# HGRN2 attention with an ELU MLP on one core: the first unit's last pair gets gates of its own, dummy products fill waits of the lead-in, and the order of the lead-in changes

## The chip, the core and the metric

The kernel runs on one core of one Trainium2 chip. The metric is device time in microseconds (us) of one execution; lower is better. The core has five engines with instruction queues of their own, each run strictly in order: TensorE (PE, with its weight loads as PEld), VectorE (DVE), ScalarE (ACT), GpSimd (POOL) and SyncE (SP), which here only starts transfers. Engines wait for each other by semaphores. Results of TensorE go to PSUM, whose banks carry names (tags) such as m0, m3, a0, a1 and h.

## The reference, cut to what matters

```python
# q, k, v, f_logit: (4 batches, 8 heads, 768 tokens, 48), fp32
f = 1.0 / (1.0 + np.exp(-f_logit))
for t in range(S):
    state = f[:, :, t, :, None] * state + np.einsum('bhd,bhe->bhde', k[:, :, t], v[:, :, t])
    y[:, :, t] = np.einsum('bhd,bhde->bhe', q[:, :, t], state)
x = y.transpose(0, 2, 1, 3).reshape(3072, 384)
h = x @ w_in                                                  # 384 x 2048, 64-bit
g = np.where(h > 0.0, h, np.exp(np.minimum(h, 0.0)) - 1.0)
out = g @ w_out                                               # 2048 x 384, 64-bit
```

A gated recurrence runs over the tokens, and its output, with the heads side by side, goes through a two-layer MLP with the ELU function between the layers.

## The kernel before

**Units.** The 3072 tokens are cut into 12 units of 256, three to a batch. A unit passes through an attention part and an MLP part; the attention of later units is strewn into the MLP of earlier ones. The eight heads are four pairs, and `NKT` = 3 is the number of the last pair.

**Attention.** `gates` turns the logits into 1 + exp(-f) on ACT; `grow` makes a running product of them with a scan on DVE, and `fall` its reciprocal on DVE (the two slots of tile `f`). `scale` multiplies k with the running product and q with the reciprocal, pair by pair, on POOL. `transposed` turns k on TensorE and has ACT copy it out; `advance` multiplies k with v into the state's increments (banks a0, a1); `step` adds up the states of the four chunks of 64 tokens; `scores` multiplies q with k, and `mask` keeps the causal half; `outputs` and `carried` (for unit 0: `first_outputs`) make the attention's result x (tile `xt`).

To spare work on the gates, the logits of pair 3 are not given a pair's room of their own: their rows fill the gaps (32 partitions) that pairs 0 to 2 leave unused, so that three pairs' instructions handle all four. `move` then copies them with two transfers inside SBUF to where pair 3 belongs: once for the running product, once for its reciprocal.

**Weights.** They arrive as 64-bit numbers, in 16 pieces of 0.79 MB (eight of w_in, eight of w_out) in the order in which they are needed: wi0, wi1, wi2, wo0, wi3, wo1, wi4, wo2, wi5, wo3 and so on. `fetch(n)` loads piece n into slot n mod 7 of the buffer `area`; a piece of w_in takes three transfers, one of w_out a single one. `split` (two DVE operations), `lower` (one on ACT) and `merge` (one on DVE) turn it into 32-bit numbers. `merge(n)` ends with `fetch(n + AHEAD)`, `AHEAD` = 7, since its slot is free then. A transfer is also issued only when the one some eight before it has landed, because they share eight semaphores in turn.

**Order.** Everything is emitted in an order written by hand, and each engine runs its instructions in that order. First comes the lead-in (L1037 to L1114): loads, the attention of unit 0 and most of the gates of unit 1. Then a loop over steps T = 0 to 191 follows. Step T, for P = T / 2, first applies the ELU of an earlier product on even steps (`elu`, for units 0 and 1), then what `at_step` has planned for T, then `up(P)` on even steps (first MLP layer, L923 for units 0 and 1, L878 from unit 2) or `down(P - 2)` on odd ones (second layer, L955 and L977), then `split` and `lower` of the piece that is merged two steps later. `A1` gives the steps of unit 1's attention: its entries are those of transposes, advance, steps, scores and mask, outputs, carried. Unit 1 has P = 6, 7, 8 between unit 0's products.

**Queue of SP.** In the lead-in SP issues, in this order: f, k, q of unit 0; f of unit 1; v of unit 0; fetch(0); k, q, v of unit 1; fetch(1); the first move of unit 1; fetches 2 to 6; then fetch(7) from merge(0). The moves of unit 0, and the second of unit 1, go out on ACT's queue.

**Dummy products.** `warm(n)` multiplies the identity with itself n times over 512 columns into bank m3; nothing reads the result. There are three at the start (`W0`) and one (`WA`) before unit 0's first `advance`. Each fp32 product is two instructions on TensorE.

Of the kernel before, what the change touches and what calls it, by code (L numbers as in the profile page):

```python
# [8 lines left out]
FP32 = mybir.dt.float32  # L9
# [347 lines left out]
def fast(ctx: ExitStack, tc: tile.TileContext, q, k, v, f_logit, w_in, w_out, out, flag, outer):  # L357
# [38 lines left out]
    WA = 1  # L396
    W0 = 3
    HOLD = 2
    A1 = (2, 4, 4, 5, 7, 9)
# [28 lines left out]
    def load(u, names="fkqv"):  # L428
        b, s0 = u // UPB, (u % UPB) * U
        for n in names.replace("v", ""):  # L430
            to = qkf[u % NB][n][MAIN]
            frm = src[n][b, :, :, s0 : s0 + U].rearrange("(p r) d s -> (r d) p s", r=2)
            if n == "f":
                to, frm = to[:, 0:NKT, 0], frm[:, 0:NKT]
            nc.sync.dma_start(out=to, in_=frm)
            for r in range(2 if n == "f" else 0):
# [14 lines left out]
    def blank(i, *engines, zeros=None):  # L451
# [4 lines left out]
        (zeros or engines[-1]).memset(qkf[i]["f"][:, NKT], 1.0)  # L456
# [114 lines left out]
    def merge(n):  # L571
        if wide and n < NFT:
# [4 lines left out]
            nc.vector.tensor_tensor(out=to.bitcast(I32), in0=bits, in1=hi, op=ALU.add)  # L577
# [67 lines left out]
    def watch(u):  # L645
        nc.vector.scalar_tensor_tensor(
            out=fine[:], in0=qkf[u % NB]["f"][:, 0:NKT, 0, U - 1 :], scalar=LIMIT, in1=fine[:],
            op0=ALU.is_le, op1=ALU.mult,
        )
# [378 lines left out]
    def warm(n):  # L1028

        pw = ps.tile([128, 4, 128], FP32, tag="m3", name="psW")  # L1030
# [6 lines left out]
    gates(0, (1, 2))  # L1037
# [4 lines left out]
    warm(W0)  # L1042
    for p in range(NKT):
        grow(0, p)
        scale(0, ("k", p, nc.gpsimd))
        if p < 2:
            transposed(0, 0, "m0", (p,))
    move(0, 0, nc.scalar)
    transposed(0, 1, "m1", (0,))
    fall(0, 0)  # L1050
    scale(0, ("q", 0, nc.gpsimd))
    warm(WA)
# [8 lines left out]
    scale(0, ("k", NKT, nc.gpsimd), ("q", 1, nc.gpsimd))  # L1061
    fall(0, 2)
    move(0, 1, nc.scalar)
    transposed(0, 1, "m1", (1,))
    advance(0, (2,))
    scores(0, None, (1,), pc)
    scale(0, ("q", 2, nc.gpsimd))
    advance(0, (3,))
    scores(0, None, (2,), pc)
# [3 lines left out]
    )  # L1073
    a = qkf[1]["f"][:, 0:NKT, 0]
# [4 lines left out]
    scale(0, ("q", NKT, nc.gpsimd))  # L1079
    scores(0, None, (NKT,), pc)  # L1080
    fall(1, 0)
    for c in range(NC - 1):
        step(0, c)
    mask(0, pc)
    step(0, NC - 1)
    split(0)
# [8 lines left out]
    for n in range(HOLD, AHEAD):  # L1095
        fetch(n)
    fall(1, 1)
    first_outputs(0)
    lower(0)
    merge(0)  # L1100
    first_outputs(1)
    scale(1, ("k", 0, nc.gpsimd), ("q", 0, nc.gpsimd), ("k", 1, nc.gpsimd), ("k", 2, nc.gpsimd))
    scale(1, ("k", NKT, nc.gpsimd))
    split(1)
    transposed(1, 0, "a0")
    transposed(1, 1, "a1")
    lower(1)
    watch(0)
    scale(1, ("q", 1, nc.gpsimd))
    fall(1, 2)  # L1110
    scale(1, ("q", 2, nc.gpsimd))
    move(1, 1, nc.scalar)
# [98 lines left out]
```

## Time and profile before

| | |
|---|---|
| median of 10 runs (lowest, highest) | 569.57 us (567.3, 571.53) |
| the profiled execution: its time; its span | 571.33 us; 569.6 us |
| granted TensorE clock, mean over the span | 0.985 |
| busy: PE, PEld | 548.1 us, 502.6 us |
| busy: DVE, ACT, POOL | 394.8, 229.5, 265.1 us |
| first up(0), up(1), up(2) start (L923) | 31.67, 35.67, 40.20 us |
| first down(0) starts (L955) | 46.81 us |
| transfers to 60 us: bytes, mean rate | 14.21 MB, 237 GB/s |

The span runs from the first to the last instruction of the profiled execution. Busy times of engines overlap. A granted clock of 0.50 means that TensorE ran at half its rate in that stretch.

### The profile page before, as it was taken

Reading aid. Unit: us, or ns where it says so; the run is one execution under the profiler, and the core shown is the slowest. Engines: PE = TensorE matmul, PEld = TensorE weight load, DVE = VectorE, ACT = ScalarE, POOL = GpSimd, SP = SyncE. Lnnn points to the kernel's source line nnn. Section 1 sums busy time; section 2 is a strip of 40 time slices with the busy share of each in tenths; the row PEclk is TensorE's granted clock in tenths of the full one; section 3 lists DMA queues with packets and bytes.
Section 4 is the critical chain, followed back from the end, with each engine's and each line's share of the span. In section 5 each row is a group of like instructions: output and inputs, shape, how many; then the busy total and the mean of one; then the engine's idle time right before and its main releaser. Section 6 shows DMA issues by size and latency. Waiting matters only on the chain.

```text
span 569.6 us, 15170 instructions
## 1 busy us (share of the span) xinstructions
PE 548.1 (96%) x6210; PEld 502.6 (88%) x6210; DVE 394.8 (69%) x765; ACT 229.5 (40%) x417; POOL 265.1 (47%) x530
## 2 busy tenths in 40 slices
PE   5588999999999999999999999999999999999996
PEld 2465777778999999999999999999999999999995
DVE  8679566745894885885785886786776876745543
ACT  3187745433433433333343343433343343233331
POOL 6510017641465456356267257257348348325332
PEclk9598999999999999999999999999999999999999
DMA  8989780061015215216216216207207203201001
GB/s 202 214 227 305 177 245 14 2 147 42 2 22 147 79 41 156 78 36 153 86 36 154 86 36 154 85 10 181 84 10 181 84 5 75 85 2 36 29 2 35
DMA packets 37902, 53.27 MB, mean 94 GB/s; under 512 B 3680, under 2 KB 27648, under 8 KB 37824
## 3 DMA queue, kind: packets, MB, share of 16 engines
q1 hardware_dynamic: 37024, 51.62, 34.8%
q8 instruction: 51, 0.84, 0.6%
q10 hardware_dynamic: 800, 0.59, 0.4%
q14 instruction: 27, 0.22, 0.1%
HBM read 44.04 MB, written 4.72 MB: 86 GB/s over the span
## 4 chain that ended last, share of the span: by engine, by line
PE 92%; DMA 4%; DVE 2%; SPq 1%; issue 0%; ACT 0%; POOL 0%; DVEq 0%; ACTq 0%; POOLq 0%
PE psH L878 35%; PE psM L977 33%; PE psM L955 8%; PE psH L923 6%; DMA area<-in_moe_w_in_dram 3%; PE psS L701 2%; PE psY L739 2%; PE psY L759 2%; PE psU_a L724 2%; PE psT L665 2%; PE psW L1032 1%; DMA f<-f 1%; ACT area L569 0%; SPq L542 0%; DVE bits L559 0%
## 5 line engine op out<-in xcount | busy, mean ns | idle before, releaser
L878 PE MATMUL psH<-xt,wi 128*128 128x128 f32 (+1 forms) x960 | 177.1, 293 | 0.0
L942 POOL TENSOR_TENSOR sums<-gg 128x128 f32<-128x128 f32 x160 | 69.6, 455 | 210.8 <-DVE gg L932 202.5
L878 PEld LDWEIGHTS psH<-xt,wi 128*128 128x128 f32 x960 | 135.9, 192 | 0.8
L910 ACT ACTIVATE gg<-hh 128x512 f32<-128x512 f32 x80 | 50.5, 631 | 205.8 <-DVE hh L900 137.9
L878 PE MATMUL psH<-xt,area 128*128 128x128 f32 x640 | 110.5, 275 | 0.0
L878 PEld LDWEIGHTS psH<-xt,area 128*128 128x128 f32 x640 | 96.9, 192 | 4.1
L887 DVE TENSOR_TENSOR hh<-psH,u 128x256 f32<-128x256 f32 x80 | 33.8, 422 | 88.7 <-ACT u L885 88.7
L977 PE MATMUL psM<-area,sums 128*128 128x192 f32 x480 | 91.2, 326 | 0.0
L977 PEld LDWEIGHTS psM<-area,sums 128*128 128x128 f32 x480 | 80.1, 190 | 0.2 <-POOL sums L942 0.2
L977 PE MATMUL psM<-wo,gg 128*128 128x192 f32 x320 | 68.1, 335 | 0.0
L617 POOL TENSOR_TENSOR k<-k,f 128x256 f32<-128x256 f32 x48 | 38.8, 811 | 60.6 <-DVE f L622 46.8
L627 DVE RECIPROCAL f<-f 128x256 f32<-128x256 f32 x36 | 62.8, 1747 | 1.3
L911 ACT ACTIVATE gg<-gg 128x512 f32<-128x512 f32 x96 | 60.6, 631 | 3.0
L932 DVE SCALAR_TENSOR_TENSOR gg<-gg,hh 128x512 f32<-128x512 f32 x80 | 55.7, 696 | 1.8 <-ACT gg L911 1.8
L977 PEld LDWEIGHTS psM<-wo,gg 128*128 128x128 f32 x320 | 50.2, 190 | 1.9
L900 DVE TENSOR_TENSOR hh<-psH,u43h 128x256 f32<-128x256 f32 (+1 forms) x160 | 49.7, 352 | 2.7
L923 PE MATMUL psH<-xt,wi 128*128 128x256 f32 x192 | 44.6, 382 | 2.3 <-DVE wi L577 1.8
L955 PE MATMUL psM<-wo,gg 128*128 128x384 f32 x128 | 46.0, 504 | 0.0
L942 POOL TENSOR_TENSOR sums<-gg,sums 128x128 f32<-128x128 f32 x80 | 42.7, 534 | 6.3
L885 ACT COPY u<-psH 128x128 f32<-128x128 f32 x80 | 21.1, 263 | 59.4 <-PE psH L878 59.4
L923 PEld LDWEIGHTS psH<-xt,wi 128*128 128x128 f32 x192 | 35.9, 190 | 9.7 <-issue 1.5
L900 DVE TENSOR_TENSOR u43h<-psH,hh 128x256 f32<-128x256 f32 x80 | 33.8, 423 | 13.4 <-PE psH L878 13.1
(97 smaller groups left out, 720.0 us busy)
## 6 DMA issues: line engine op xcount, KB each, us to landing
area<-in_moe_w_out_dram SPq DMA_DIRECT2D x8, 768.0 KB, 8.0
again<-in_moe_w_in_dram SPq DMA_DIRECT2D x16, 384.0 KB, 4.1
again<-in_moe_w_out_dram SPq DMA_DIRECT2D x16, 384.0 KB, 3.5
k<-in_k_dram SPq DMA_DIRECT2D x12, 384.0 KB, 4.8
q<-in_q_dram SPq DMA_DIRECT2D x12, 384.0 KB, 5.9
v<-in_v_dram SPq DMA_DIRECT2D x12, 384.0 KB, 6.3
area<-in_moe_w_in_dram SPq DMA_DIRECT2D x8, 576.0 KB, 7.8
out_dram<-o SPq DMA_DIRECT2D x38, 96.0 KB, 1.7
```

The source lines that it names most:

```text
L617: e.tensor_tensor(out=t[n][:, p], in0=t[n][:, p], in1=t["f"][:, p, "kq".index(n)], op=ALU.mult)
L627: nc.vector.reciprocal(f[:, p, 1], f[:, p, 0])
L878: nc.tensor.matmul(to, lhsT=lhs, rhs=rhs, start=(n == 0), stop=True, skip_group_check=True)
L887: add = lambda to, x, y: nc.vector.tensor_tensor(out=to, in0=x, in1=y, op=ALU.add)
L900: add = lambda to, x, y: nc.vector.tensor_tensor(out=to, in0=x, in1=y, op=ALU.add)
L910: nc.scalar.activation(g[:], h, AF.Relu, scale=-1.0)
L911: nc.scalar.activation(g[:], g[:], AF.Exp, scale=-1.0)
L923: nc.tensor.matmul(ph[:, i], lhsT=wi[j][:, kt, i * 128 : (i + 1) * 128], rhs=xts[m][:, kt, :], start=(kt == 0), stop=(kt == NKT - 1),)
L932: nc.vector.scalar_tensor_tensor(out=g[:], in0=g[:], scalar=-1.0, in1=phs.pop(P), op0=ALU.add, op1=ALU.max)
L942: nc.gpsimd.tensor_tensor(out=s[:, i], in0=x, in1=y, op=op)
L955: nc.tensor.matmul(pm[t][:], lhsT=g[:, i, t * 128 : (t + 1) * 128], rhs=wo[:, 2 * j + i, :], start=(j == 0 and i == 0), stop=(j == NP - 1 ...
L977: nc.tensor.matmul(pm[bank][:, half * DH : (half + 1) * DH], lhsT=x, rhs=y, start=first, stop=(j == NP - 1), skip_group_check=True,)
```

## The change

Four things change, all in the lead-in and in the first steps of the loop.

1. Unit 0's logits of pair 3 are loaded into that pair's own place, in one transfer with the others; POOL fills the tile with 50.0 ahead of it. The four moves of unit 0 go; there is a fourth `grow` and a fourth `fall`, and `gates` works in pieces of 1, 1 and 2 pairs. `watch_last` extends a range check to pair 3.
2. `warm` takes a bank as argument, and calls of one product are put ahead of the scores of pairs 1, 2 and 3, behind the scores of pair 3, and behind `first_outputs`.
3. The order: `split`, `lower` and `merge` of piece 0 go ahead of unit 1's gates, around `mask(0)`, and with the merge its fetch(7) goes ahead of fetches 2 to 6. Unit 1's bias, scans and first move go behind `mask(0)`. Piece 1 is split and merged inside the lead-in. Unit 1's transposes and last gates move from the lead-in to step 1 of the loop, its last q to step 4, and its state steps, scores and outputs one to two steps later (`A1`).
4. The merges of pieces 3 to 15 run on POOL instead of DVE (`M0`).

```diff
--- before.py
+++ after.py
@@ -394,9 +394,11 @@
     LAG = 2
     AHEAD = 7
     WA = 1
+    M0 = 3
+    Q1 = 4
     W0 = 3
     HOLD = 2
-    A1 = (2, 4, 4, 5, 7, 9)
+    A1 = (2, 4, 5, 7, 8, 9)
     D2 = (14, 16, 18, 20)
     A2 = (22, 24, 24, 26, 27, 28)
     D3 = (-7, -5, -3, -1)
@@ -430,10 +432,12 @@
         for n in names.replace("v", ""):
             to = qkf[u % NB][n][MAIN]
             frm = src[n][b, :, :, s0 : s0 + U].rearrange("(p r) d s -> (r d) p s", r=2)
-            if n == "f":
+            if n == "f" and u:
                 to, frm = to[:, 0:NKT, 0], frm[:, 0:NKT]
+            elif n == "f":
+                to = to[:, :, 0]
             nc.sync.dma_start(out=to, in_=frm)
-            for r in range(2 if n == "f" else 0):
+            for r in range(2 if n == "f" and u else 0):
                 nc.sync.dma_start(
                     out=qkf[u % NB][n][GAP[r] : GAP[r] + PAD, 0:NKT, 0],
                     in_=src[n][b, 2 * NKT + r, :, s0 : s0 + U].rearrange("(i j) s -> i j s", i=PAD),
@@ -453,7 +457,10 @@
             w = HP // len(engines)
             for n in "kq":
                 e.memset(qkf[i][n][:, j * w : (j + 1) * w], 0.0)
-        (zeros or engines[-1]).memset(qkf[i]["f"][:, NKT], 1.0)
+        if i:
+            (zeros or engines[-1]).memset(qkf[i]["f"][:, NKT], 1.0)
+        else:
+            engines[-1].memset(qkf[i]["f"][:, :, 0], 50.0)
 
     start = ctx.enter_context(ExitStack())
     start.enter_context(tc.manual_schedule())
@@ -574,7 +581,8 @@
             j, out_ = parts[n]
             to = wo[:, 2 * j : 2 * j + 2] if out_ else wi[j][:]
             bits, hi = (x.rearrange("p (k f) -> p k f", k=to.shape[1]) for x in (held.pop(n)[:], hi))
-            nc.vector.tensor_tensor(out=to.bitcast(I32), in0=bits, in1=hi, op=ALU.add)
+            e = nc.gpsimd if n >= M0 else nc.vector
+            e.tensor_tensor(out=to.bitcast(I32), in0=bits, in1=hi, op=ALU.add)
         fetch(n + AHEAD)
 
 
@@ -645,6 +653,12 @@
     def watch(u):
         nc.vector.scalar_tensor_tensor(
             out=fine[:], in0=qkf[u % NB]["f"][:, 0:NKT, 0, U - 1 :], scalar=LIMIT, in1=fine[:],
+            op0=ALU.is_le, op1=ALU.mult,
+        )
+
+    def watch_last(u):
+        nc.vector.scalar_tensor_tensor(
+            out=fine[:, 0:1], in0=qkf[u % NB]["f"][:, NKT:, 0, U - 1 :], scalar=LIMIT, in1=fine[:, 0:1],
             op0=ALU.is_le, op1=ALU.mult,
         )
 
@@ -1025,31 +1039,28 @@
         nc.tensor.matmul(pf[0:1, :], lhsT=low[:], rhs=causal[:, W - 1 : W], start=True, stop=True)
         nc.vector.tensor_copy(flag[:], pf[0:1, :])
 
-    def warm(n):
-
-        pw = ps.tile([128, 4, 128], FP32, tag="m3", name="psW")
+    def warm(n, bank="m0"):
+
+        pw = ps.tile([128, 4, 128], FP32, tag=bank, name="psW")
         for _ in range(n):
             nc.tensor.matmul(
                 pw[:], lhsT=ident[:], rhs=ident[:].unsqueeze(1).broadcast_to([128, 4, 128]), start=True, stop=True
             )
 
 
-    gates(0, (1, 2))
+    gates(0, (1, 1, 2))
     fetch(0)
     load(1, "kqv")
     for n in range(1, HOLD):
         fetch(n)
-    warm(W0)
-    for p in range(NKT):
+    warm(W0, "m3")
+    for p in range(HP):
         grow(0, p)
         scale(0, ("k", p, nc.gpsimd))
-        if p < 2:
-            transposed(0, 0, "m0", (p,))
-    move(0, 0, nc.scalar)
-    transposed(0, 1, "m1", (0,))
+        transposed(0, p // 2, f"m{p // 2}", (p % 2,))
     fall(0, 0)
     scale(0, ("q", 0, nc.gpsimd))
-    warm(WA)
+    warm(WA, "m3")
     gates(1, bias=0)
     advance(0, (0, 1))
     pc = scores(0, ("m2", "m3"), (0,))
@@ -1058,32 +1069,37 @@
         vs[0][:, :, PAD : PAD + NKT * 2 * D].rearrange("t w (p r d) -> t w p r d", r=2, d=D)[:, :, :, 0],
     )
     fall(0, 1)
-    scale(0, ("k", NKT, nc.gpsimd), ("q", 1, nc.gpsimd))
+    scale(0, ("q", 1, nc.gpsimd))
     fall(0, 2)
-    move(0, 1, nc.scalar)
-    transposed(0, 1, "m1", (1,))
+    fall(0, 3)
     advance(0, (2,))
+    warm(1)
     scores(0, None, (1,), pc)
     scale(0, ("q", 2, nc.gpsimd))
     advance(0, (3,))
+    warm(1)
     scores(0, None, (2,), pc)
     nc.gpsimd.tensor_copy(
         padded_v[:, :, :, PAD : 2 * PAD].rearrange("t w (r j) k -> t w r j k", r=2),
         vs[0][:, :, PAD + NKT * 2 * D : PAD + DM].rearrange("t w (r k j) -> t w r j k", r=2, j=NKT),
     )
+    scale(0, ("q", NKT, nc.gpsimd))
+    warm(1)
+    scores(0, None, (NKT,), pc)
+    warm(1)
+    split(0)
+    for c in range(NC - 1):
+        step(0, c)
+    lower(0)
+    mask(0, pc)
+    merge(0)
+    step(0, NC - 1)
     a = qkf[1]["f"][:, 0:NKT, 0]
     nc.vector.tensor_scalar_add(a, a, 1.0)
     for p in range(NKT):
         grow(1, p)
     move(1, 0, nc.sync)
-    scale(0, ("q", NKT, nc.gpsimd))
-    scores(0, None, (NKT,), pc)
-    fall(1, 0)
-    for c in range(NC - 1):
-        step(0, c)
-    mask(0, pc)
-    step(0, NC - 1)
-    split(0)
+    split(1)
     for c in range(NC - 1):
         nc.gpsimd.tensor_copy(
             padded_s[:, c, :, PAD : 2 * PAD],
@@ -1094,28 +1110,29 @@
         nc.gpsimd.memset(area[:, HOLD:].bitcast(I32)[:, :, 0:1], 0)
     for n in range(HOLD, AHEAD):
         fetch(n)
+    first_outputs(0)
+    first_outputs(1)
+    warm(1)
+    lower(1)
+    fall(1, 0)
+    scale(1, ("k", 0, nc.gpsimd), ("k", 1, nc.gpsimd), ("k", 2, nc.gpsimd), ("q", 0, nc.gpsimd))
     fall(1, 1)
-    first_outputs(0)
-    lower(0)
-    merge(0)
-    first_outputs(1)
-    scale(1, ("k", 0, nc.gpsimd), ("q", 0, nc.gpsimd), ("k", 1, nc.gpsimd), ("k", 2, nc.gpsimd))
+    merge(1)
     scale(1, ("k", NKT, nc.gpsimd))
-    split(1)
-    transposed(1, 0, "a0")
-    transposed(1, 1, "a1")
-    lower(1)
     watch(0)
-    scale(1, ("q", 1, nc.gpsimd))
-    fall(1, 2)
-    scale(1, ("q", 2, nc.gpsimd))
-    move(1, 1, nc.scalar)
-    watch(1)
-    at_step(1, lambda: scale(1, ("q", NKT, nc.gpsimd)))
+    watch_last(0)
+    at_step(1, lambda: transposed(1, 0, "a0"), lambda: transposed(1, 1, "a1"))
+    at_step(1, lambda: scale(1, ("q", 1, nc.gpsimd)))
+    at_step(1, lambda: fall(1, 2))
+    at_step(1, lambda: scale(1, ("q", 2, nc.gpsimd)))
+    at_step(1, lambda: move(1, 1, nc.scalar))
+    at_step(1, lambda: watch(1))
+    at_step(Q1, lambda: scale(1, ("q", NKT, nc.gpsimd)))
     attention(1, (), A1)
     for n in range(1, NFT):
         t = max(needs[n][0] - 2, 0)
-        at_step(t, lambda n=n: merge(n))
+        if n > 1:
+            at_step(t, lambda n=n: merge(n))
         if n > 1:
             later.setdefault(max(t - 2, 0), []).append(n)
     at_step(4, lambda: load(2))
```

## The prediction

> **What bounds the kernel now.** I read the page's slices first, then the chain of waits over the first 70 us, then the timeline and the windows of that stretch, and last who waited for whom on SP's queue.
>
> ```profile
> PE   5588999999999999999999999999999999999996
> PEclk9598999999999999999999999999999999999999
> ```
>
> ```profile
> 16.80:30.00 13.20, 9.96 (x250) 8.23 (x250) 7.66 (x12) 2.95 (x5) 7.30 (x14) 0.50 0.98 230
> 30.00:46.80 16.80, 12.10 (x176) 9.71 (x172) 14.07 (x25) 15.11 (x16) 1.47 (x2) 1.00 0.88 232
> ```
>
> A slice is 14.2 us. TensorE is full from the fifth slice to the last but one, so a change in the first 47 us moves the end only by what it moves the point from which TensorE no longer stops. Inside those 47 us it stops often, and the windows (columns: PE, PEld, DVE, ACT, POOL busy, granted clock, DMA share, GB/s) say that from 16.8 to 30 us it ran at half its clock.
>
> ```profile
> 10.33 5.31 DMA f<-f
> 16.01 9.73 DMA area<-in_moe_w_in_dram
> 29.17 6.28 DMA area<-in_moe_w_in_dram
> 36.67 1.97 ACT area L569
> 46.88 4.47 PE psM L955 x8
> ```
>
> ```profile
> 16.81 0.69 PE L665 MATMUL psT<-ident,k 128*128 128x128 f32 x2 [4.10 <-POOL k L617]
> 19.71 0.72 POOL L617 TENSOR_TENSOR q<-q,f 128x256 f32<-128x256 f32 x1 [1.20 <-DMA f<-f]
> 20.48 0.71 PE L701 MATMUL psS<-q,k 64*64 64x64 f32 x16 [1.06 <-POOL q L617]
> 21.31 1.29 DVE L709 TENSOR_TENSOR at<-psS,twice 128x512 f32<-128x512 f32 x2 [1.19 <-PE psS L701]
> 31.67 2.86 PE L923 MATMUL psH<-xt,wi 128*128 128x256 f32 x12 [0.53 <-ACT xt L816]
> 35.67 2.83 PE L923 MATMUL psH<-xt,wi 128*128 128x256 f32 x12 [1.14 <-DVE wi L577]
> 40.20 2.83 PE L923 MATMUL psH<-xt,wi 128*128 128x256 f32 x12 [0.63 <-DVE wi L577]
> ```
>
> Two chains meet here. The attention of unit 0 ends in its first MLP product, up(0), at 31.67; it lost time to the two copies of gates inside SBUF (f<-f): TensorE idles 4.10 us for pair 3's k, and pair 3's q comes only at 19.71. The second chain is the supply of weights: fetch, split (DVE), lower (ACT), merge (DVE). up(1) and up(2) wait for a merge, and the first down only starts at 46.81.
>
> **What the Trainium skill says.** "TensorE: Matmul & The Clock Gate", part 1, says that the array falls to half its clock after an idle window of about 3.4 us and needs as long a busy one to recover. The trace agrees on the first half (clock 1.00 to 15 us, an idle stretch of 4.10 us, then 0.50); on the second it took longer, full only at about 30. "GPSIMD Engine Reference", section 3.1, puts a two-input operation at about twice VectorE's time. Here POOL takes 0.455 us for 128x128 and 0.73 for 128x256, so by an estimate on that line 0.455 + 5 x 0.275 = 1.8 us for a merge's 768 elements, against 0.95 on DVE: agreed. "DMA: Bandwidth & Descriptors", section "Anatomy of one DMA", has a fixed cost near 2 us for each transfer, worked out there for POOL's path; the 48 KB gate transfers took 3.0 us at the quiet start, 5.3 inside the loaded stretch.
>
> **Start of unit 0.** The old gate load wrote pairs 0 to 2 and waited for nothing (issued at 0.80; the last of its three pieces landed at 4.8). The new one writes all four pairs, over an area that POOL now fills with 50.0. That memset stands third on POOL, behind k and q, from 1.72; it has 1024 columns where the old had 512 (0.49 us), so it ends near 2.7. Cost: the load goes at 2.73. k, q and the next f follow on SP, about 0.5 us later than now, as two issues (1.33 us) fall away. k took 4.6 us to land with others beside it, so I take 3.8 for f: 6.5. Bounds 5.8 and 7.5. The gates start 1.7 us later than now (4.84).
>
> Then by rows: exponent and bias 0.42 each, pairs 2 and 3 0.61 and 0.63, so ACT ends at 9.6; the four scans (0.69) end at 10.9 instead of 8.65. Four reciprocals at 1.65 (three took 4.94) run to 17.5. Pair 3 costs DVE 0.69 + 1.65 = 2.3 us more, on the path, and the two pairs of copies go: pair 3's k is there at 11.7 instead of 16.8, its q at 17.5 + 0.73 = 18.2 instead of 20.4. Its scores end near 18.9 instead of 21.2.
>
> **The dummy products.** One takes two passes: 5.49 / 3 = 1.8 us each at the cold start, 1.02 at 10.26. Each stands where TensorE waits for the next q, which comes every 1.65 us; advance and scores of a pair need some 0.7 us at full clock. So those ahead of pairs 1 and 2 fit; the one ahead of pair 3 ends near 18.6, 0.4 us after its q, which is hidden because DVE is not free for the mask before 19.4; the one behind has until the mask is done. The last takes the cover that unit 1's transposes had beside ACT's copies of xt (0.48 + 0.96 us). I cost all at nothing; if the clock is half, each overruns by up to 1 us. What they buy is the clock: 64-column products took 1.16 us for 64 at full clock (L739), 0.71 for 16 at half.
>
> **To up(0).** DVE: split(0) 17.5 to 18.6 (now ahead of the mask: 1.1 us on the path), two steps 0.75, mask 1.3, to 20.7. First outputs part 0: 96 products, now 22.06 to 26.88, at full clock 96 x 1.16 / 64 = 1.75 us, 2.0 with the next weights, behind the second mask: 22.7; part 1's 76 products 1.4 and ACT's copy between them 0.3, to 24.4 (now 30.1); xt 1.45 later, at 25.9. up(0) starts at 25.95 instead of 31.67, 5.7 us earlier. At half clock it would be 29.8.
>
> **The queue of SP.** merge(0) now stands ahead of the loop that fetches 2 to 6, and merge(0) itself issues fetch(7). So SP reaches fetch(7) first and waits there for merge(0), at 21.6; behind it stands the move of unit 1's gates, which waits for unit 1's scans, now behind the mask: 24.9; behind that fetches 2 to 6, which went from 21.06 on. The waits of SP's queue show that it stops like this:
>
> ```profile
> SPq L542 <- DMA f<-f: 8.1, 2, 7.8
> SPq L540 <- DVE wi L577: 3.3, 2, 3.1
> ```
>
> Cost: fetch(2) is issued at 26.3. The fetches before it are limited by bandwidth (some 240 GB/s): 4.72 MB from 4.5 us are in at 24.3, fetch(7)'s 0.79 MB at 27.8, the move at 29, fetch(2) at 31.5 instead of 29.7, and each further one 3.3 us later: fetch(3) 34.8, (4) 38, (5) 41.3, (6) 44.6, (8) 47.9. Part is given back: now SP stood still from 30.4 to 38.2, and fetch(6) landed at 43.9, (8) at 50.6.
>
> **From up(0) on.** merge(1) follows fall(1,0) and fall(1,1) on DVE: 30.4; pair 3's k of unit 1 follows the move: 29.9. TensorE is queued behind the transposes (1.1 us), so up(1) goes at 30.6 instead of 35.67. up(2): fetch(2) 31.5, split 1.1, lower 1.95 to 34.5, merge behind split(3) and elu(0): 37.55, start 37.6 instead of 40.2. down(0): merge(3), on POOL, 40.8, so down(0) runs 40.9 to 43.6 behind up(2) (now 46.81 to 51.3, part of it at half clock). up(3): fetch(4) 38, split 39.1, lower 42, POOL merge 44, start 44.1 (now 51.35). Then scores of unit 1, moved from step 5 to 7, which wait for the steps on DVE to free their banks: 47.6 to 48.7, down(1) to 51.4, mask and outputs to 52.9, up(4) 55.4, carried 56.5, down(2) 59.3, up(5) 61.9. Now up(5) ends at 66.86: **5.0 us less**.
>
> The 13 merges moved to POOL cost 0.85 us of latency each and free DVE 0.95 each. POOL is idle from 40 to 75 us, and the merges stood 5 to 7 us ahead of their use, so I cost them at nothing; near 90 us, where POOL is full of mixes, two merges push unit 2's scales by up to 4 us, which its transposes (95.1, scales ready at 91.0) just cover. Uncovered, 1 us. The extra check of pair 3 (L646, 0.1 us) hides in DVE's slack. Bounds of the total: if only the weight supply decided and it were 2 us later than above, 3 us; if no stall of mine (6.7 us between up(0) and up(5)) occurred, 11.7 us less; half of that seems the most.
>
> The sum is against the profiled span, 569.6, with 1.7 us around it (571.33). The median of the runs shown is 569.57; minus 5.0 gives 564.6.
>
> **Rivals.**
> 1. Likeliest, 0.50: as summed, 563.0 to 566.5, taken at 564.6.
> 2. The weights decide, 0.20: attention is early, but fetch(2) lands 3 us later than I put it, and TensorE waits in up(2) and up(3). For it: SP's new order; DMA is at 0.9 to 1.1 of its share all along. Against: the hole from 36 to 39 us (134 GB/s). Gain 2, 567.6.
> 3. Fewer stalls than mine, 0.08: DVE, freed of merges, keeps up; gain 8, 561.6.
> 4. Nothing, 0.08: the late gate load and the fourth reciprocal eat the copies' gain, and the clock falls all the same; 569.
> 5. Slower, 0.14: SP's head of line. fetch(2) must wait for merge(0), fetch(7) and the scans. up(3) breaks even if fetch(2) lands at 38.8, 7 us later than I say; at 42, which takes a mask 5 us late and transfers queued behind it, the run ends 3 us later: 572.6. For it: fetch(1) took 9.7 us to land. Against: merge(0) depends on nothing of the slow DMAs.
>
> The run can tell about 0.3%, 1.7 us, from no change. Case 2 gives 0.02 of its chance to no change: faster 0.50 + 0.18 + 0.08 = 0.76, same 0.08 + 0.02 = 0.10, slower 0.14. Range 561.3 to 570.5: it leaves out most of case 5 and the end of case 3.
>
> **What would show it.** Right: no f<-f on ACT before 30 us; clock 1.00 from 16 to 30; up(0) near 26; in SP's queue the w_out fetch ahead of fetch(2). Wrong: fetch(2) landing after 35, TensorE waiting for wi longer than now, up(5) ending after 65, or gaps near 95 us behind POOL.

## The result, and the profile after

| | before | after |
|---|---|---|
| median of the runs, us | 570.20 (31 runs) | 575.32 (9 runs) |
| lowest and highest, us | 567.30, 571.53 | 574.03, 576.94 |
| profiled execution: its time, its span, us | 571.33, 569.6 | 575.85, 574.1 |
| up(5) ends at, us (behind it TensorE hardly stops in either) | 66.86 | 71.58 |

The ratio is 1.0096 with a 95% interval of 1.0082 to 1.0111: the changed kernel is slower by 5.1 us between the medians, 5.5 by the ratio. The forecast was 564.6. The end of up(5) comes 4.7 us later and the span is 4.5 us longer, so the loss lies wholly before that point, in the lead-in and the first steps of the loop, where the gain had been looked for. (Lines move by 8 in the upper part of the changed kernel and by 14 in the lower: up is L937, down L969, the merge L585.)

The slices of the page after, TensorE and its clock:

```profile
PE   5969899999999999999999999999999999999996
PEclk8898999999999999999999999999999999999998
```

A slice is 14.4 us. TensorE's second went from 5 to 9 and its clock from 5 to 8, as intended; but the third fell from 8 to 6 and the fifth, 57 to 72 us, from 9 to 8. The windows of the lead-in say more. Columns: from and to, PE, PEld, DVE, ACT, POOL busy with their instructions, granted clock, DMA share, GB/s.

```profile
17.00:30.00 13.00, 11.97 (x277) 7.24 (x270) 10.59 (x16) 3.90 (x7) 5.57 (x10) 0.96 0.71 182
30.00:48.00 18.00, 13.01 (x108) 10.25 (x107) 15.22 (x19) 10.95 (x11) 5.91 (x6) 0.83 0.91 229
```

The half clock of before is gone from most of the first stretch (0.96; before 0.50 from 16.8 to 30); it now lies earlier, from about 11 to 18 us, where before the clock was at 1.00 to about 16. But the transfers there ran at 182 GB/s instead of 230, and from 30 to 48 us the mean clock is 0.83 (before 1.00 from 30 to 46.8). A finer set of windows of the same trace shows where the transfers stopped:

```profile
21.00:24.00 3.00, 2.85 (x32) 1.13 (x30) 1.40 (x3) 0.78 (x1) 0.09 (x2) 1.00 0.69 150
24.00:27.00 3.00, 2.61 (x130) 2.31 (x132) 2.93 (x6) 0.33 (x2) 0.18 (x1) 1.00 0.37 80
30.00:33.00 3.00, 2.89 (x17) 2.34 (x15) 3.00 (x3) 2.60 (x3) 0.93 (x2) 1.00 0.49 104
```

80 GB/s from 24 to 27 us, and 104 from 30 to 33, while the weights are what the MLP waits for. What SP waited for (engine, line, releaser, us, times, longest):

```profile
SPq L547 <- DVE state L696: 8.4, 1, 8.4
SPq L642 <- DVE f L630: 3.2, 1, 3.2
```

SP stands 8.4 us at L547, which is fetch(7), until merge(0) is through (the page names the neighbouring step on DVE), then 3.2 us at L642, the move of unit 1's gates, for the scans of L630. Only then fetch(2) goes, at 30.45. The chain of waits from there on (start, us, what) shows who was waiting for the weights:

```profile
30.45 0.53 SPq L549
...
32.97 9.47 DMA area<-in_moe_w_in_dram
...
42.45 6.15 DMA area<-in_moe_w_in_dram
48.60 1.83 POOL wi L585
...
50.46 2.19 DVE bits L566
...
52.67 0.58 DVE area L570
...
53.27 1.93 ACT area L576
...
55.27 2.04 POOL wi L585
```

Two things are seen. The weights are late; and behind them stands a train in which a merge on POOL (1.83), a split on DVE (2.19 for its first half instead of 0.56) and the next lower and merge follow one another: the engine that was to be relieved waits for the one that relieves it (DVE stood 2.75 us for POOL ahead of 50.46). TensorE's timeline of the same kernel (start, us, what, and in brackets the idle time before and who ended it):

```profile
14.00 1.91 PE L1046 MATMUL psW<-ident 128*128 128x512 f32 x2
...
20.96 1.12 PE L1046 MATMUL psW<-ident 128*128 128x512 f32 x2
22.02 0.46 PE L715 MATMUL psS<-q,k 64*64 64x64 f32 x16
...
29.37 2.86 PE L937 MATMUL psH<-xt,wi 128*128 128x256 f32 x12 [0.49 <-ACT xt L830]
...
34.56 2.83 PE L937 MATMUL psH<-xt,wi 128*128 128x256 f32 x12 [0.58 <-DVE wi L585]
40.42 0.31 PE L738 MATMUL psU_a<-v,kn 64*64 64x48 f32 x2 [3.03 <-ACT kn L683]
...
42.61 5.49 PE L937 MATMUL psH<-xt,wi 128*128 128x256 f32 x12 [0.56 <-DVE wi L585]
...
50.89 2.75 PE L937 MATMUL psH<-xt,wi 128*128 128x256 f32 x12
54.45 1.59 PE L715 MATMUL psS<-q,k 64*64 64x64 f32 x64 [0.81 <-PE psH L937]
...
60.05 0.33 PE L753 MATMUL psY<-at,v 64*64 64x64 f32 x2 [1.22 <-DVE at L723]
```

up(0) starts 2.3 us earlier than before (31.67), up(1) 1.1 (35.67); then TensorE stops 3.03 us for kn, which ACT copies behind lower(2), for which ACT stood idle 4.51 us until piece 2 was split; the clock falls, and up(2) takes 5.49 us instead of 2.83. In the kernel before, unit 1's scores stood ahead of up(3):

```profile
45.72 1.16 PE L701 MATMUL psS<-q,k 64*64 64x64 f32 x62 [0.21 <-DVE state L682]
...
51.19 2.75 PE L923 MATMUL psH<-xt,wi 128*128 128x256 f32 x12
```

So up(3), at 50.89, is still 0.3 us early, but the scores, now at 54.45, are still owed: the kernel is behind.

### The profile page after: what moved, and what is told of

It reads as the page before. It is cut to its first block, busy times and chain, and to the rows that moved or that the text cites. A ratio compares the mean times of both kernels' runs of the same rounds, so it can differ in the third digit from the quotient of the medians.

```text
span 574.1 us, 15184 instructions
## 1 busy us (share of the span) xinstructions
PE 553.1 (96%) x6220; PEld 503.7 (88%) x6220; DVE 394.0 (69%) x755; ACT 229.9 (40%) x419; POOL 292.3 (51%) x543
## 4 chain that ended last, share of the span: by engine, by line
PE 89%; DMA 3%; DVE 2%; POOL 2%; issue 1%; ACT 1%; SPq 1%; DVEq 0%; POOLq 0%; ACTq 0%
PE psH L892 34%; PE psM L991 32%; PE psM L969 6%; PE psH L937 5%; DMA area<-in_moe_w_in_dram 3%; PE psS L715 2%; PE psU_a L738 2%; PE psY L773 2%; PE psY L753 2%; PE psT L679 2%; PE psW L1046 1%; DMA f<-in_f_logit_dram 1%; POOL wi L585 1%; POOL k L625 1%; DVE bits L566 0%
## 5 line engine op out<-in xcount | busy, mean ns | idle before, releaser
L635 DVE RECIPROCAL f<-f 128x256 f32<-128x256 f32 x37 | 64.2, 1745 | 1.0
L937 PE MATMUL psH<-xt,wi 128*128 128x256 f32 x192 | 47.4, 399 | 1.6 <-DVE wi L585 1.1
L937 PEld LDWEIGHTS psH<-xt,wi 128*128 128x128 f32 x192 | 37.5, 199 | 10.0 <-ACT xt L830 1.3
L969 PE MATMUL psM<-wo,gg 128*128 128x384 f32 x128 | 44.6, 492 | 0.0
```

Source lines behind the costliest of these rows:

```text
L635: nc.vector.reciprocal(f[:, p, 1], f[:, p, 0])
L937: nc.tensor.matmul(ph[:, i], lhsT=wi[j][:, kt, i * 128 : (i + 1) * 128], rhs=xts[m][:, kt, :], start=(kt == 0), stop=(kt == NKT - 1),)
L969: nc.tensor.matmul(pm[t][:], lhsT=g[:, i, t * 128 : (t + 1) * 128], rhs=wo[:, 2 * j + i, :], start=(j == 0 and i == 0), stop=(j == NP - 1 ...
```

## The experiments

Times are medians; each ratio is to runs of the kernel before on the same chip, with its 95% interval. Six runs (e1, e2, e4, e6, e9, e13) rest on four executions each. "The changed kernel" is 1.0096.

| run | made from | median, us | ratio | interval |
|---|---|---|---|---|
| e1_fetch_first | changed; fetches 2 to 5 first | 576.44 | 1.0109 | 1.0077 to 1.0142 |
| e9_after_fetch23 | changed; fetches 2, 3 first | 574.09 | 1.0055 | 1.0034 to 1.0076 |
| e2_merges_dve | changed; merges on DVE | 575.07 | 1.0090 | 1.0060 to 1.0121 |
| e3_both | e1 and e2 | 572.55 | 1.0060 | 1.0042 to 1.0077 |
| e6_both_late_transposes | e3, transposes at step 3 | 575.20 | 1.0093 | 1.0073 to 1.0112 |
| e4_no_dummies | changed; no new dummies | 574.43 | 1.0086 | 1.0056 to 1.0115 |
| e11_old_steps | changed; `A1` as before | 573.97 | 1.0065 | 1.0039 to 1.0091 |
| e5_before_pool_merges | before; merges on POOL | 570.55 | 1.0011 | 0.9998 to 1.0025 |
| e7_own_gates_only | before; own gates | 570.93 | 1.0018 | 1.0008 to 1.0027 |
| e14_old_order_dve | e7 and dummies | 570.64 | 1.0022 | 1.0013 to 1.0032 |
| e10_parts_without_order | e14 and POOL merges | 573.06 | 1.0040 | 1.0022 to 1.0059 |
| e8_two_fetches_first | e9 and e2, one dummy less | 571.42 | 1.0033 | 1.0014 to 1.0053 |
| e12_best_try | e8, other steps | 569.55 | 0.9988 | 0.9977 to 0.9998 |
| e15_best_old_queue | e12 with the changed SP order | 572.26 | 1.0055 | 1.0032 to 1.0077 |
| e13_best_pool | e12 with POOL merges | 573.55 | 1.0084 | 1.0059 to 1.0110 |
| e17_pool_four_bits | e13, four `bits` buffers | 572.48 | 1.0039 | 1.0027 to 1.0050 |
| e18_best_four_bits | e12, four `bits` buffers | 569.49 | 0.9988 | 0.9978 to 0.9998 |
| e16_best_no_dummies | e12 without its dummies | 569.39 | 1.0006 | 0.9994 to 1.0017 |

**The order on SP.** My theory after the result was that fetch(7) and the move hold up fetches 2 to 6. The first edit puts four fetches ahead of the move and fetch(7) last:

```diff
+    for n in range(HOLD, 6):
+        fetch(n)
     scale(0, ("q", NKT, nc.gpsimd))
...
-    merge(0)
+    merge(0, False)
...
-    for n in range(HOLD, AHEAD):
+    for n in range(6, AHEAD + 1):
```

`merge(n, more=True)` calls its fetch only when `more` holds; a small memset of `area` that stands ahead of the loop moves up with it.

> The changed kernel, but fetches 2 to 5 are issued ahead of split(0), and fetch(7) goes behind fetch(6) as before. Theory A (SP's order starves the weights: fetch(2) left at 30.45 us behind the gates' move, and the DMA engines ran at 80 to 200 GB/s from 21 to 33 us): fetch(2) lands before 28, up(2) starts 4 us or more earlier than 42.6, and the time falls 4 to 8 us below the changed kernel's 575.3, to 567 to 571, a ratio to before of 0.995 to 1.002. Theory B (the merges on POOL are what costs): at most 2 us less, ratio 1.006 or more. Theory C (the dummy products are on the path): little change, 1.008 to 1.010.

It gained nothing: 1.0109, where theory A had 0.995 to 1.002. TensorE's timeline of this run shows a new wait in the old one's place:

```profile
39.59 0.69 PE L680 MATMUL psT<-ident,k 128*128 128x128 f32 x2 [6.25 <-DVE gg L947]
```

The page names DVE, but what came last was POOL's k of pair 3 (38.58 to 39.54), and POOL had stood 5.34 us for the move: the transpose needs the moved gates. Their two 48 KB transfers took 9.1 us behind four fetches of 0.79 MB, where the changed kernel's, on nearly idle queues, took 2.7 (issue to landing). So weights and gates compete, and the order must serve both. The next edit is the same with `range(HOLD, 4)` and `range(4, AHEAD + 1)`: two pieces, the move, then the rest.

> The changed kernel with one thing altered: SP issues fetches 2 and 3 ahead of split(0), then the gates' move, then fetches 4 to 7. Merges on POOL and all dummies stay. Theory A (SP's order is the main cost): fetch(2) lands near 25 instead of 36.7, the move by 31, up(2) starts 2 us or more earlier than 42.61, and the time is 2.5 to 5 us below the changed kernel's 575.3: ratio 1.001 to 1.005. If the order of SP counts only together with DVE's merges: ratio 1.006 to 1.009.

1.0055, between the two ranges expected, and the interval lies below the changed kernel's: 0.41% or 2.3 us back. fetch(2) goes at 17.95 and up(2) runs from 41.35 at full clock (2.86 us); but the train of POOL is still there:

```profile
41.35 2.86 PE L938 MATMUL psH<-xt,wi 128*128 128x256 f32 x12 [0.56 <-DVE wi L585]
...
48.12 2.86 PE L938 MATMUL psH<-xt,wi 128*128 128x256 f32 x12 [1.33 <-POOL wi L585]
```

The same part taken back from the mended kernel e12 (below) is the reverse test: e15 is e12 without these lines.

> As e12_best_try, with SP's order as in the changed kernel: fetch(7) and the gates' move ahead of fetches 2 to 6. Theory A: fetch(2) lands near 36 again, and the time is 3 to 5 us above e12, ratio 1.004 to 1.008. If SP's order counted only through what followed it in the loop: within 2 us of e12.

It costs 1.0055 against 0.9988, 0.67% or 3.8 us, as expected, and up(2) runs at half clock again:

```profile
40.68 4.92 PE L937 MATMUL psH<-xt,wi 128*128 128x256 f32 x12
```

The SP order is a cause in both directions: taken out of the changed kernel it gives 2.3 us, put into e12 it costs 3.8. The time contains what it does to the clock of up(2); no run parts the two.

**The merges on POOL.** In the changed kernel they go back to DVE with one constant, in the kernel before they go to POOL with one line:

```diff
-    M0 = 3
+    M0 = 16
```

> The changed kernel with all merges on DVE (M0 = 16). Theory A: the weights still come late, so 0 to 1.5 us less than the changed kernel: ratio 1.007 to 1.010. Theory B (a merge takes 1.85 us on POOL instead of 0.95, and the splits on DVE beside it take 2.1 instead of 0.56): 3 to 5 us less, ratio 1.000 to 1.004. Theory C: no change.

> The kernel before, with the merges of pieces 3 to 15 on POOL and nothing else changed. Theory B (POOL's merges cost by themselves: 1.85 us instead of 0.95, and a split beside one takes 2.1 instead of 0.56): 1.5 to 4 us longer than before, ratio 1.003 to 1.007. Theory A (only the order counts): within 0.3% of before.

Both say: nearly nothing, 0.06% and 0.11%, each within its interval (e2's is 0.3% to either side, 1.7 us). Taken alone that would acquit them. e3, with both edits of e1 and e2, gives a first doubt, since the sum is worth 0.36%, more than the two parts (-0.13% and 0.06%), though the intervals of e1 and e2 are too wide to show that it is more:

> Both: fetches 2 to 5 first, and all merges on DVE. Theory A: as e1_fetch_first, or up to 1 us better or worse. Theory B: as e2_merges_dve or 1 us better. If both count, the gains add up: 6 to 10 us less than the changed kernel, ratio 0.992 to 0.998.

In e3 TensorE still waits 6.71 us for POOL's k behind the move. The test is made in e12, where the weights are on time: e13 is e12 with `M0 = 3`.

> As e12_best_try (569.55, ratio 0.9988), with the merges of pieces 3 to 15 back on POOL. Theory B' (POOL's merges cost little while DVE waits for weights anyway, as between the changed kernel and e2, and much once the weights are there, as between e9 and e8): 2 to 4 us above e12, ratio 1.002 to 1.006, with splits on DVE near 1.1 us for their second operation. Against it: within 1 us of e12.

1.0084 against 0.9988: 0.96% or 5.5 us, more than I expected of it, and the largest single difference measured here, though from four executions. The groups of DVE between 28 and 72 us (count, busy us, mean ns, idle before and its releasers), of e12:

```profile
L570 DVE TENSOR_SCALAR area<-area 128x768 int32<-128x768 int32 x11 | 7.0, 636 | 0.4
L566 DVE TENSOR_SCALAR bits<-area 128x768 int32<-128x768 int32 x10 | 5.6, 558 | 0.2
```

and of e13:

```profile
L566 DVE TENSOR_SCALAR bits<-area 128x768 int32<-128x768 int32 x11 | 11.5, 1044 | 3.4 <-POOL wi L585 3.3
L570 DVE TENSOR_SCALAR area<-area 128x768 int32<-128x768 int32 x11 | 8.7, 789 | 0.4
```

The two operations of a split took 12.6 us together (21 of them), now 20.2 (22), and DVE stood another 3.3 for POOL: a merge on POOL frees its `bits` buffer late, and there are two. Do the long splits cost the time, or the wait for a buffer? Four buffers take away the wait alone:

```diff
-        bits = held[n] = sb.tile([128, 2 * DM], I32, tag="bits", name=f"bits{n}")
+        bits = held[n] = sb.tile([128, 2 * DM], I32, tag="bits", name=f"bits{n}", bufs=4)
```

(`again` in `reread`, which shares the tag, likewise.)

> The mended version with 13 merges on POOL (1.0084 of the kernel before) and four `bits` buffers in place of two. Theory A, the merges hold DVE up by freeing the two buffers late: DVE no longer waits for POOL ahead of a split (it waited 3.3 us), and most of the 5.5 us comes back: 568 to 571, ratio below 1.003. Theory B, POOL's instructions stretch DVE's splits (0.56 to about 2 us) and are themselves 0.9 us longer than DVE's merge: the wait for POOL goes, the splits stay near 1 us in the mean and the ratio stays above 1.005.

> The control: the mended version with its merges on DVE and four `bits` buffers. DVE waits for no buffer there with two, so both theories expect no change from 0.9988: 0.997 to 1.001.

The control is unchanged at 0.9988. With POOL's merges the ratio falls from 1.0084 to 1.0039, between the ranges of the two theories. The 2.9 us between e17 and its control e18 (22 and 14 executions, on one chip, intervals apart) are what the merges on POOL cost without a wait for buffers. Part of it goes with the clock: the executions of the two at 0.992 or more have medians of 570.5 and 569.5 us. The other 2.6 us, between e13 and e17, are less certain than their intervals say, for the granted clock differs between executions. All four of e13 had a mean clock of 0.984 to 0.987, and a median of 573.55 us. e17's ran from 0.986 to 0.995; its ten at 0.986 or 0.987 have a median of 573.6, no less than e13's, and its seven at 0.992 or more 570.5. The profiles show how this comes about. TensorE's last pauses ahead of up(2) are the same in e12 and in e13 (0.56 and 0.17 us beside these):

```profile
36.87 0.31 PE L739 MATMUL psU_a<-v,kn 64*64 64x48 f32 x2 [1.41 <-ACT kn L684]
```

```profile
37.94 0.31 PE L739 MATMUL psU_a<-v,kn 64*64 64x48 f32 x2 [1.40 <-ACT kn L684]
...
40.12 4.39 PE L938 MATMUL psH<-xt,wi 128*128 128x256 f32 x12 [0.56 <-DVE wi L585]
```

but in e13 the clock fell and up(2) took 4.39 us, where e12's and e17's took 2.86. The fall (0.92 from 39 to 40 us, 0.50 from 40 to 42) came before the first merge on POOL, which began at 40.68. So whether the buffers are worth 2.6 us or the four executions of e13 happened to draw the low clock is open; that DVE no longer waits for POOL with four is seen. Where at least part of the 2.9 us comes from is seen in e17, whose DVE group shows no wait and long splits:

```profile
L570 DVE TENSOR_SCALAR area<-area 128x768 int32<-128x768 int32 x11 | 10.1, 919 | 0.4
L566 DVE TENSOR_SCALAR bits<-area 128x768 int32<-128x768 int32 x10 | 10.0, 1002 | 0.0
```

**Own gates and dummies.** Part one alone, in the order of before: pair 3's load, four scans, four reciprocals, no moves for unit 0, and the check.

```diff
-        if p < 2:
-            transposed(0, 0, "m0", (p,))
-    move(0, 0, nc.scalar)
-    transposed(0, 1, "m1", (0,))
+        transposed(0, p // 2, f"m{p // 2}", (p % 2,))
...
     fall(0, 2)
-    move(0, 1, nc.scalar)
-    transposed(0, 1, "m1", (1,))
+    fall(0, 3)
```

> The kernel before with part 1 alone: pair 3's logits of unit 0 in their own place, its scan and reciprocal, no moves of unit 0; order, dummies and merges as before. If the gates of its own pay (my working: pair 3's q 2 us earlier, and no idle stretch of 4.1 us, so the clock stays up): up(0) 1 to 5 us earlier than 31.67, time 1 to 4 us below before, ratio 0.993 to 0.998. If the later load and DVE's 2.3 us more eat it: ratio 0.998 to 1.004. If part 1 is what makes the change slow: above 1.005.

It is 0.18% slower, not faster. TensorE no longer waits for a move; it waits for the mask instead:

```profile
23.47 0.48 PE L815 MATMUL psY<-at,even_v 64*64 64x64 f32 x4 [4.10 <-DVE at L720]
```

The same 4.10 us, by chance of the digits: DVE has a scan and a reciprocal more, and in the old order unit 1's scans and its first reciprocal stand ahead of the mask, which starts at 22.73 (before: 21.31). Its clock also fell, to 0.50 from 12 to 18 us and again from 22, against the first case of the expectation. With four of the new dummies added in the old order, and then POOL's merges too:

> As e10_parts_without_order (573.06, ratio 1.0040) with all merges on DVE: the old order with gates of its own and four dummies. If POOL's merges made what e10 lost beyond e7: as e7, ratio 1.000 to 1.002. If the dummies made it: ratio 1.003 or more.

> The kernel before with the gates of its own, four of the dummy products and the merges on POOL, but in the old order (part 3 left out). If the new order holds most of the loss: as the sum of e7 and e5, 1 to 2 us above before, ratio 1.001 to 1.004. If the parts cost together what none costs alone (dummies on the path, POOL beside DVE): ratio 1.006 or more.

The dummies change nothing there (1.0018 to 1.0022), POOL's merges add 0.18% (the intervals overlap); all parts without the new order cost 0.40%, so that 0.56% of the changed kernel's 0.96% comes with the order, its steps and the fifth dummy. Then the changed kernel without its five new dummies (each `warm(1)` behind `fall(0, 3)`):

> The changed kernel without its five new dummy products of the lead-in (those at the start and before the first advance stay). Theory C (the three ahead of scores are on the path: pair 3's q is ready at 19.2 us, its scores start at 22.0): the mask starts 1.5 us or more earlier than 22.6, up(0) 1.5 us earlier than 29.37, and the time falls 1 to 3 us, ratio 1.005 to 1.008. Theory A: up(0) may move but the time does not, as up(2) waits for its weights: ratio 1.008 to 1.010. What the dummies are for: without them the granted clock falls to 0.5 between 17 and 30 us, up(0) starts no earlier than now, and the time is the same or longer.

The mask comes at 19.98 instead of 22.60, and 21 to 31 us run at half clock; the ratio, 1.0086, differs from 1.0096 by less than the intervals. Its first MLP product:

```profile
30.84 4.55 PE L937 MATMUL psH<-xt,wi 128*128 128x256 f32 x12 [1.55 <-ACT xt L830]
```

4.55 us at half clock where the changed kernel takes 2.86 from 29.37 on. The dummies give the clock and take 2.6 us of the path to the mask for it. In the mended order, e12 without its four:

> As e12_best_try without the four dummies that it keeps. If they are worth their place once their delay of the scores is gone: up(0) 1 us or more later than 28.60, clock 0.5 for some of 20 to 31 us, the time 0.5 to 2.5 us above e12, ratio 1.000 to 1.003. If the time hangs on weights and DVE alone: within 0.5 us of e12 or below.

1.0006 against 0.9988, or 1.0 us: the intervals overlap, and their far ends are 2.3 us apart. The median of e16, 569.39, is no longer than e12's, at a lower clock (0.979 to 0.988, e12 0.989 to 0.997). So the dummies raise the clock, and what that is worth is 1 us, if anything.

**The steps.** Unit 1's attention steps back to where they were:

```diff
-    A1 = (2, 4, 5, 7, 8, 9)
+    A1 = (2, 4, 4, 5, 7, 9)
```

> The changed kernel with unit 1's state steps, scores, outputs and carried at their old steps of the loop (A1 as before). TensorE stood 3.8 us after up(3) in the changed kernel, in front of scores, outputs and carried of unit 1, as DVE's steps and mask were late. If the later steps made that: 2 to 4 us less than the changed kernel, ratio 1.003 to 1.006. If the weights made it (DVE held up by splits that wait for POOL): within 1 us of it, or longer, as scores come earlier than DVE can serve them.

1.0065; against the changed kernel 0.31% or 1.8 us, just short of what was expected if the steps made the stop, and the intervals overlap. Moving unit 1's transposes from step 1 to step 3 on top of e3 was meant to remove the stall on the moved gates:

> As e3_both, with unit 1's transposes at step 3 instead of step 1. In e3_both TensorE stood 6.7 us in front of the fourth pair's transpose, since the gates' move lay behind fetches 2 to 5 and landed at 37.7 us; up(1) was queued behind it. If that wait took the place of the one removed, up(1) starts at 33 to 34 instead of 39.0, up(2) at 39 to 42 instead of 44.9, and the time falls 2 to 5 us below e3_both's 572.6: ratio 0.997 to 1.003. If DVE's later work (steps, mask) decides, it stays within 1 us of e3_both.

It did not: up(1) comes earlier (34.43 instead of 39.02), at half clock (4.51 us), then advance waits 4.88 us for ACT's kn, and the ratio is 1.0093.

**A mended version.** e8 combines e9's order with merges on DVE and drops the dummy ahead of the last pair's scores; e12 has, beside that, these two edits:

```diff
-    A1 = (2, 4, 5, 7, 8, 9)
+    A1 = (2, 4, 4, 6, 8, 9)
...
-    at_step(4, lambda: load(2))
+    at_step(9, lambda: load(2))
```

> The changed kernel with all merges on DVE, fetches 2 and 3 ahead of split(0), then the gates' move, then fetches 4 to 7, and without the dummy product ahead of the last pair's scores. If the weights and the move compete for SP and the DMA engines, this order serves both: fetch(2) lands near 25, the move near 29 to 31, up(1) at 32 to 33, up(2) at 37 to 39, and the time is 4 to 8 us below the changed kernel's 575.3, ratio 0.994 to 1.002. If DVE's order (steps and mask of unit 1 late) decides, ratio 1.004 to 1.008.

> As e8_two_fetches_first, with unit 1's state steps at 4 and scores at 6 (mask ahead of outputs by two steps), and the load of unit 2 at step 9 instead of 4, behind the transfer of unit 1's x. In e8 TensorE stood 2 us before outputs, for the mask, and 1.1 us at 67.5 for that transfer. If these are what is left: 1.5 to 4 us below e8's 571.4, ratio to before 0.996 to 1.001.

e8 is at 1.0033, between its two ranges. e12 and its twin e18 are the only ones below the kernel before: 0.9988, by the interval 0.0023 below at the most. The two further edits of e12 were not tried apart. It keeps the first part, four of five dummies and most of the new order, and still wins about 0.7 us, 1.3 at the most. Its lead-in has up(0) at 28.60, 0.8 us ahead of the changed kernel, and from there is on time:

```profile
32.63 2.83 PE L938 MATMUL psH<-xt,wi 128*128 128x256 f32 x12 [0.30 <-DVE wi L585]
...
39.05 2.86 PE L938 MATMUL psH<-xt,wi 128*128 128x256 f32 x12 [0.56 <-DVE wi L585]
```

Single profiles have to be read with care here: e12's span is 3.2 us shorter than that of the profile before, and the medians differ by 0.5. The profile before was one of the slower executions of its kernel (571.33 against 570.20, clock 0.985), and e12's the lowest of its 22 (568.27, clock 0.997).

## Why the prediction was wrong

The mechanism of loss stood in the prediction as rival 5, "Slower, 0.14: SP's head of line", at 572.6; the likeliest case had the same chain with other numbers. It was right in kind only: by its own bound (fetch(2) landing at 38.8) the landing near 36.7 would have cost nothing. In the changed kernel two terms of the sum failed: the dummies at nothing (most of why the mask came 3.2 us late, and fetch(2), which waits behind it on SP, 4.2), and the path behind up(0) with every engine free when the late piece 2 arrives (TensorE stopped 3.03 us and then ran up(2) 2.7 us longer). A third, the merges on POOL at nothing, failed in the mended order. By its own steps:

| step | predicted, us | measured, us |
|---|---|---|
| f of unit 0 landed | 6.5 | 6.96 |
| fourth scan ends | 10.9 | 11.65 |
| fourth reciprocal ends | 17.5 | 18.2 |
| last scores of unit 0 end | 18.9 | 22.48 |
| mask starts | 19.4 | 22.60 |
| fetch(2) issued | 26.3 | 30.45 |
| up(0) | 25.95 | 29.37 |
| up(1) | 30.6 | 34.56 |
| up(2) | 37.6 | 42.61 |
| down(0) | 40.9 | 47.89 |
| up(3) | 44.1 | 50.89 |
| up(5) ends | 61.9 | 71.58 |

- *Start of unit 0*: right in kind, 0.7 us short, most of it in f's landing. What it left out is that TensorE stood through much of the later start (busy 1.02 of the 3 us from 8 to 11), and the clock was 0.50 from about 11 to 18 us.
- *The dummy products*, "I cost all at nothing": wrong, and the first step that failed. WA's products ran at half clock (1.91 us for two passes, where the prediction had 1.02) until 15.9, so advance began then. From there each pair's scores wait for the dummy ahead of them, 1.06 to 1.2 us each; the last scores ended 3.6 us late: pair 3's q was there at 19.2, and its scores began at 22.02, so 2.8 us of it are the dummies' and the rest the later start. I had set the dummies against the 1.65 us between two reciprocals, but TensorE entered that stretch late and never caught up. e4 confirms it: without them the mask comes 2.6 us earlier (the run is no faster, as the clock falls and up(0) comes at 30.84). That they keep the clock up was right, from 18 us on.
- *To up(0)*: 5.7 us of gain predicted, 2.3 had; the difference is in the two items above.
- *The queue of SP*: the mechanism was right (fetch(7), move and then fetch(2)), the size wrong: 26.3 was built on merge(0) at 21.6 and unit 1's scans at 24.9, which ended at 24.76 and 28.39. Both follow the mask, which came 3.2 us late. The bound set for a loss, "up(3) breaks even if fetch(2) lands at 38.8", is a second error. Piece 2 was in near 36.7 (its first split starts at 36.80), and up(3) did come 0.3 us earlier than before; but unit 1's scores, 1.6 us, which stood ahead of up(3) before, were still to come. Behind up(3) it stopped 0.81, 1.22, 0.27 and 0.29 us more, where before it did not stop at all.
- *From up(0) on*: this step took each engine for free when the weights arrive. Not foreseen was that kn of unit 1 stands behind lower(2) on ACT, so that a late piece 2 stops advance too (3.03 us), and that the clock fell behind this pause: up(2) took 5.49 us, 2.7 more than at full clock. In e9, with piece 2 on time, it took 2.86.
- *The 13 merges moved to POOL*, "I cost them at nothing": wrong in e12's order. They were to cost 0.85 us of latency each and to free DVE. The latency was right (1.84 to 2.1 us against 0.95), but DVE is not freed. There the term is 2.9 us with four buffers (e17, e18) and 5.5 with two (e13), of which the clock may have made a part. In the changed kernel taking it back alone showed 0.06% (e2). That other stops hide it there, the late weights first, is an argument and not shown: e8, which is e9 with the merges back on DVE and a dummy less, is only 0.22% below it, and their intervals overlap.
- The range's upper end, 570.5, left out most of rival 5. The rival counted the late weights and no second loss behind them.

From runs, the 0.96% splits as: own gates 0.18% (e7), dummies 0.04% (e14), POOL's merges 0.18% (e10), the order with its steps 0.56% (the rest). Of these the first and the last are clear of their intervals. This sum holds in the order it was taken; e2, e9, e13 and e15 show that the parts hide each other.

Left open: how the 2.9 us of e17 divide between POOL's latency, DVE's longer splits and the clock; how much of e13's further 2.6 us is the buffers' and how much the clock's; why e6 lost what it gained at up(1); and whether near 90 us, where the prediction saw a risk, two merges on POOL push unit 2's scales. No stop of TensorE shows there, and nothing was tried for it.

## What to carry to other kernels

Before an instruction is pulled ahead, list what it issues, its transfers above all, and put on the issuing queue first what is waited for first; a small transfer with a late input neither belongs ahead of the large ones nor behind all of them. Work moved to an idle engine is not free if the two engines meet in a buffer or in memory: count the time until its inputs' buffers are released, and look at how long the other engine's instructions take beside it. When two causes hide each other, removing one shows little; take the mended version and put each back. And look at the granted clock of each execution before a difference of a few us is put down to an edit.

## What the runs showed of the hardware

**In e17 a DVE split that began while a merge ran on POOL ended after it.** There, between 39 and 60 us, five splits began while a merge ran on POOL. Three of them, DVE's timeline of e17:

```profile
39.94 2.22 DVE L566 TENSOR_SCALAR bits<-area 128x768 int32<-128x768 int32 x1
...
46.15 2.20 DVE L566 TENSOR_SCALAR bits<-area 128x768 int32<-128x768 int32 x1
...
57.55 2.15 DVE L570 TENSOR_SCALAR area<-area 128x768 int32<-128x768 int32 x1
```

and POOL's of the same kernel:

```profile
39.55 2.20 POOL L585 TENSOR_TENSOR wo<-bits,area 128x768 int32<-128x768 int32 x1 [2.47 <-ACT area L576]
...
45.97 1.95 POOL L585 TENSOR_TENSOR wo<-bits,area 128x768 int32<-128x768 int32 x1
...
57.44 1.84 POOL L585 TENSOR_TENSOR wi<-bits,area 128x768 int32<-128x768 int32 x1 [2.46 <-ACT area L576]
```

The splits end at 42.16, 48.35 and 59.70, the merges at 41.75, 47.92 and 59.28: 0.41 to 0.43 us later each time, which is most of a split's own 0.56. The split at 39.46, begun before the merge, kept its 0.56, and that merge took 2.20 instead of 1.85. As these lines read, the two take turns, and the first to start goes first. The profile before had a sign of it, beside POOL's scales:

```profile
22.35 1.52 POOL L617 TENSOR_TENSOR k<-k,f 128x256 f32<-128x256 f32 x2
```

```profile
23.21 1.08 DVE L559 TENSOR_SCALAR bits<-area 128x768 int32<-128x768 int32 x1
```

POOL ended at 23.87, and the split 0.42 us later. The prediction priced both operations of a split at 1.1 us together, which is what they take with POOL idle. The Trainium skill's "GPSIMD Engine Reference", section 8, names a cause that fits: POOL shares its SBUF interfaces with VectorE and contends with DVE instructions that run in a 2-port mode or have two SBUF inputs. The splits have one input each, so it would have to be the mode, which no run here shows. The prediction took POOL's price from that page and left this sentence out.

**The clock fell without one long pause.** In e4 TensorE ran at half clock from 21 to 31 us. Ahead of the fall its timeline shows pauses of 0.84 and 1.21 us; from 17 to 21 us it was busy 1.95 of 4 us (the number behind the length):

```profile
17.00:21.00 4.00, 1.95 (x92) 1.67 (x86) 3.93 (x7) 1.87 (x2) 2.56 (x7) 0.93 1.09 271
```

The Trainium skill's "TensorE: Matmul & The Clock Gate", part 1, speaks of an idle window of about 3.4 us, and also of a kernel whose frequent short pauses made the clock swing; this looks like the second. The dummies kept the clock at 1.00 through the same stretch, and bought nothing that the medians can show. Nor do the last pauses alone decide: e12 and e13 had the same ahead of up(2), and the clock fell in one of them. The prediction also read the slow return of the clock before the change as a difference from the page. But TensorE had pauses there until 27.19, and 2.8 us later, at 30.0, the clock was full; this trace does not speak against the page.

**A small transfer's time depends on what is under way.** Two 48 KB copies inside SBUF took 2.7 us to land in the changed kernel, with the DMA share at 0.33 from 28 to 30 us and 0.49 from 30 to 33, and 9.1 us in e1, behind four pieces of 0.79 MB.
